# Pooled scores on quarters of the array, eight weight parts' low halves on TensorE, and a planner that counts GpSimd's hold

## The chip, the cores and the metric

The program runs on one core of one Trainium2 chip. The metric is the device time of one execution in microseconds; before the change the median of three runs is 743.98 us (743.76 to 744.39). The core has five engines with an in-order instruction queue each: TensorE (PE in the profile; its weight loads are PEld), VectorE (DVE), ScalarE (ACT), GpSimd (POOL) and SyncE (SP), which here only issues DMA transfers.

## The reference

Two stages, all in float32; some weights come as float64. Stage one is attention for 8 batches of 8 heads, 576 positions, head size 64. Each head does it twice and adds the results:

```python
q_d = q.reshape(B, H, Sd, factor, D).mean(axis=3)      # factor 4, Sd = 144; k_d, v_d alike
out_up = np.repeat(sm_attn(q_d, k_d, v_d), factor, axis=2)
mask = np.abs(pos[:, None] - pos[None, :]) < factor    # local: seven keys around each query
out_local = np.matmul(softmax(where(mask, scores, -1e9)), v)
return out_up + out_local
```

Stage two is a channel mix on x, the heads side by side (512 wide), with x_prev one position earlier:

```python
xk = mu_k * x + (1 - mu_k) * x_prev                    # xr the same with mu_r
k = np.maximum(xk @ w_k, 0); v = (k * k) @ w_v         # 512 -> 1024 -> 512
return sigmoid(xr @ w_r) * v
```

## The kernel before, in words

**Pairs.** Attention goes by 32 pairs of heads, n = 0 to 31, four to a batch; the two heads (e = 0, 1) lie in partitions 0 to 63 and 64 to 127. For a pair `turn_q` (L296) and `turn_k` (L305) transpose the raw queries and keys on VectorE. The keys go into `kz`, two planes that are zero where the other head lies, so `turn_k` is two transposes of 64 partitions, and one matmul with 128 rows gives both heads' local scores side by side. `pool_q`, `pool_k` and `pool_v` (L312 to L332) add groups of four positions on GpSimd.

**Scores.** Local scores (`ps_s`, L343) are 24 small f32 matmuls, for 24 blocks of 24 queries against 32 keys; for the first eight pairs (`PEM`) the mask is first written by a matmul with the identity (L340), later VectorE adds it. Pooled scores (`ps_d`, L400) are 144 x 144 a head, in three tiles of 64 queries a head starting at 0, 64 and 80 (`T0`); the third overlaps. Each is a matmul of 64 rows and 64 columns, head 0 on the upper left quarter of the array and head 1 on the lower right. Maxima and sums are VectorE's, exponentials ScalarE's, normalising is GpSimd's. `down_turn` (L435, L436) transposes the pooled weights on TensorE through `att` banks, `down_copy` (L444, L446) copies them out, and `av_pe` (L457, L463) multiplies by the values. `spread` (L393) fills the local weights into `bd`. From pair 5 on `run_pe` issues the values of pair n-1 and the scores of pair n as one block. The `att` ring has two banks, used by `ps_s`, `ps_d` and `ps_t`.

**Chunks.** Stage two goes by 18 chunks of 256 positions. Every product is split: an operand is a high part, rounded to fp32r, and a low part, the rest, and three products (high x high, low x high, high x low) are added. For a chunk c the mixing (`diff` L515, `mix_part`, `mix_add` L540) makes xk, `mix_high` (L544) and `mix_low` (L549) split it into `xkh` and `xkl`, `k_pe` (L557) makes eight slices `ps_g` of k, ScalarE squares them and takes the high part `kh` (L569), `k_low` (L576) makes `kl` on VectorE or GpSimd (GpSimd for chunk 0 and for slices 1, 3 and 5, `KLF`), `r_pe` (L588) makes the gate and `v_pe` (L606) the second product.

**Weights.** Twenty parts of 128 x 512 arrive as float64, 512 KB each, into staging tiles borrowed from later buffers. ScalarE scales the upper word (L224), VectorE makes a float32 of both words in three integer operations (L229, L233, L238), ScalarE rounds the high part (L242), and `weight_low` (L247) subtracts it: ten parts on VectorE (`LOWDVE`), ten on GpSimd.

**Order.** Nothing is left to a scheduler. Each step is given to `Plan.add` with its engine, a duration in us, a rank (roughly a due time, from `PER`, `STEP0`, `STEP1`, `W0`, `WSTEP`, `XLEAD`, `MIXED`), what it reads and writes, and the ring it takes a buffer from. `Plan.order` plays the steps on that model: of the steps that could start first on an engine it takes the lowest rank. The order that results is fixed on every engine. The durations in it only choose an order; they are no measurement.

Of the kernel before, what the change touches and what calls it, by code (L numbers as in the profile page):

```python
# [154 lines left out]
def attention_moe(ctx: ExitStack, tc, q, k, v, mu_k, mu_r, w_k, w_v, w_r, band, ident, out):  # L155
# [85 lines left out]
    def weight_high(i):  # L241
        nc.scalar.activation(weight_part(WORDER[i])[1], part32[i], AF.Copy)  # L242

# [54 lines left out]
    def turn_k(n):  # L298

        d = st[n]  # L300
        d["kz"] = kz = kzs[n % 2]
        raw = d["kraw"].rearrange("p c d -> p (c d)")
        for e in range(2):
            h = slice(64 * e, 64 * e + 64)
            nc.vector.transpose(kz[h, e, 3:579], raw[h])  # L305
# [21 lines left out]
    def pool_v(n):  # L327
# [4 lines left out]
        nc.gpsimd.tensor_tensor(out=vd, in0=v4[:, :, 0:64], in1=v4[:, :, 64:128], op=ALU.add)  # L332
        d["vd"] = vd

    def score_pe(n):
        d = st[n]
        qT, kz = d["qT"], d["kz"]
        ps = pp.tile([P, NG, 2, 32], F32, tag="att", name="ps_s", bufs=AB)
        if n < PEM:
            nc.tensor.matmul(ps, idn, mask[:, :, None, :].broadcast_to([P, NG, 2, 32]), start=True, stop=False)  # L340
        for j in range(4 * NG):
            g, i = divmod(j, 4)
            nc.tensor.matmul(ps[32 * i:32 * i + 32, g, :, :], qT[:, QT * j:QT * j + 32],  # L343
                             kz[:, :, QT * j:QT * j + 32], start=(n >= PEM), stop=(n >= PEM or g == NG - 1))
        d["ps_s"] = ps

    def score_top(n):
        d = st[n]
# [4 lines left out]
        if n < PEM:
            p3 = ps.rearrange("p g e c -> p (g e) c")
            nc.vector.tensor_reduce(out=mx, in_=p3, axis=AX.X, op=ALU.max)
            nc.vector.tensor_tensor(out=s3, in0=p3, in1=mx[:, :, None].broadcast_to([P, 12, 32]),
                                    op=ALU.subtract)
        else:
            nc.vector.tensor_tensor(out=sm, in0=ps, in1=mask[:, :, None, :].broadcast_to([P, NG, 2, 32]),
                                    op=ALU.add)  # L360
            nc.vector.tensor_reduce(out=mx, in_=s3, axis=AX.X, op=ALU.max)
        d.update(s3=s3, mx=mx)
# [31 lines left out]

    def down_pe(n):
        d = st[n]
        ps = pp.tile([P, 3, 144], F32, tag="g" if n < NP else "att", name="ps_d", bufs=2)
        for t in range(3):
            for e in range(2):
                nc.tensor.matmul(ps[64 * e:64 * e + 64, t, :], d["qd"][64 * e:64 * e + 64, T0[t]:T0[t] + 64],  # L400
                                 d["kd"][64 * e:64 * e + 64, :], start=True, stop=True)
        d["ps_d"] = ps

    def down_top(n):
        d = st[n]
# [1 line left out]
        nc.vector.tensor_reduce(out=mx, in_=d["ps_d"], axis=AX.X, op=ALU.max)
# [458 lines left out]
```

## Time and profile before

| | |
|---|---|
| median of three runs | 743.98 us |
| the profiled execution | 744.03 us |
| its span, first to last instruction | 742.2 us |
| mean granted TensorE clock | 0.958 |
| PE, DVE, ACT, POOL busy | 664.1, 479.7, 454.5, 332.9 us |
| DMA | 62.14 MB, mean 84 GB/s |

A row of a group reads: line, engine, operation, output and inputs by the program's names, shapes, count, then busy time and mean duration in ns of one, then the idle time of the engine ahead of it and what ended that. In the chain a row is a start, a length and a line; "x12" counts records, and an f32 matmul leaves two.

### The profile page before, as it was taken

The page shows a single profiled execution, that of the slowest core. Times are in us where ns is not written, and L with a number is a line of the kernel's source. Part 1 is how long each engine was busy: PE and PEld are TensorE (multiplying, and loading weights), DVE is VectorE, ACT ScalarE, POOL GpSimd, SP SyncE. Part 2 cuts the span into 40 slices and gives each one's busy share as a digit, 9 for nine tenths or more (in the row PEclk, how much of TensorE's full clock was granted, in tenths as well). Part 3 has the DMA queues.
Part 4 walks back from the last instruction along what each step waited for, and adds up shares of the span by engine and source line. Part 5 has one row for each costly group of instructions (what it writes and reads, how often), then busy time and mean ns, then how long its engine had stood idle before and what let it go on. Part 6 is the DMA issues. An engine that isn't in the chain of part 4 may idle for free.

```text
span 742.2 us, 17757 instructions
## 1 busy us (share of the span) xinstructions
PE 664.1 (89%) x7008; PEld 569.1 (77%) x7008; DVE 479.7 (65%) x839; ACT 454.5 (61%) x1150; POOL 332.9 (45%) x400
## 2 busy tenths in 40 slices
PE   2651777789999999999999999999999999999997
PEld 2441655668788878887888888887888788888886
DVE  3679879856885596559845387829782975175111
ACT  1365656557775767576765567657765776564432
POOL 6634547546565464543434255636563653010100
PEclk9975878799999999999999999999999999999999
DMA  9999765354336243623234143544353100000000
GB/s 136 177 236 162 174 145 138 51 130 85 87 73 127 50 99 67 123 57 79 46 86 99 39 91 59 119 54 103 66 119 59 58 2 30 1 30 29 1 28 29
DMA packets 221845, 62.14 MB, mean 84 GB/s; under 512 B 205122, under 2 KB 214594, under 8 KB 221762
## 3 DMA queue, kind: packets, MB, share of 16 engines
q1 hardware_dynamic: 221762, 61.01, 39.1%
q8 instruction: 55, 0.90, 0.5%
q14 instruction: 28, 0.23, 0.1%
HBM read 51.55 MB, written 9.44 MB: 82 GB/s over the span
## 4 chain that ended last, share of the span: by engine, by line
PE 79%; DVE 8%; DMA 3%; issue 3%; SPq 3%; ACT 2%; POOL 1%; DVEq 0%; POOLq 0%; ACTq 0%
PE ps_g L557 27%; PE acc L606 23%; PE ps_r L588 14%; PE ps_v L463 3%; PE ps_s L343 3%; PE ps_d L400 3%; PE ps_v L457 2%; SPq L259 2%; DMA qraw<-in_q_dram 2%; PE ps_t L435 1%; DVE xkl L549 1%; DVE w L238 1%; DMA stg<-in_moe_w_k_dram 1%; DVE w L233 1%; DVE xk L540 1%
## 5 line engine op out<-in xcount | busy, mean ns | idle before, releaser
L557 PE MATMUL ps_g<-xkh,wkh 128*128 128x256 f32 x576 | 167.0, 290 | 13.3 <-ACT xkh L544 11.1
L557 PE MATMUL ps_g<-xkl,wkh 128*128 128x256 f32 x576 | 164.8, 286 | 15.7 <-DVE xkl L549 15.7
L557 PE MATMUL ps_g<-xkh,wkl 128*128 128x256 f32 x576 | 163.7, 284 | 0.0
L576 POOL TENSOR_TENSOR kl<-kk,kh 128x256 fp32r<-128x256 f32 x59 | 46.9, 796 | 224.2 <-ACT kh L569 174.4
L576 DVE TENSOR_TENSOR kl<-kk,kh 128x256 fp32r<-128x256 f32 x85 | 46.9, 552 | 149.6 <-ACT kh L569 143.9
L557 PEld LDWEIGHTS ps_g<-xkl,wkh 128*128 128x128 f32 x576 | 111.0, 193 | 21.3 <-DVE xkl L549 17.8
L562 ACT ACTIVATE kk<-ps_g 128x256 f32<-128x256 f32 x144 | 55.1, 382 | 116.9 <-PE ps_g L557 110.4
L557 PEld LDWEIGHTS ps_g<-xkh,wkh 128*128 128x128 f32 x576 | 111.1, 193 | 18.8 <-ACT xkh L544 11.3
L606 PE MATMUL acc<-wvh,kh 128*128 128x512 f32 x288 | 116.3, 404 | 0.0
L606 PE MATMUL acc<-wvh,kl 128*128 128x512 f32 x288 | 114.0, 396 | 1.5 <-DVE kl L576 1.5
L606 PE MATMUL acc<-wvl,kh 128*128 128x512 f32 x288 | 113.8, 395 | 1.6 <-POOL wvl L247 1.0
L557 PEld LDWEIGHTS ps_g<-xkh,wkl 128*128 128x128 f32 x576 | 111.2, 193 | 0.0
L606 PEld LDWEIGHTS acc<-wvh,kl 128*128 128x128 f32 x288 | 54.2, 188 | 15.5 <-DVE kl L576 2.3
L393 ACT ACTIVATE bd<-at 32x288 f32<-32x288 f32 x128 | 56.2, 439 | 14.8 <-DVE at L386 13.2
L569 ACT ACTIVATE kh<-kk 128x256 fp32r<-128x256 f32 x144 | 60.2, 418 | 4.7 <-PE acc L606 0.2
L568 ACT ACTIVATE kk<-kk 128x256 f32<-128x256 f32 x144 | 60.1, 418 | 4.4
L606 PEld LDWEIGHTS acc<-wvl,kh 128*128 128x128 f32 x288 | 54.3, 189 | 10.8 <-POOL wvl L247 1.3
L606 PEld LDWEIGHTS acc<-wvh,kh 128*128 128x128 f32 x288 | 54.2, 188 | 9.7 <-issue 0.2
L588 PE MATMUL ps_r<-wrh,xrh 128*128 128x512 f32 x144 | 57.2, 397 | 0.0
L588 PE MATMUL ps_r<-wrh,xrl 128*128 128x512 f32 x144 | 56.9, 395 | 0.0
L588 PE MATMUL ps_r<-wrl,xrh 128*128 128x512 f32 x144 | 56.8, 395 | 0.0
L323 POOL TENSOR_TENSOR tk<-kz 64x288 f32<-64x288 f32 x64 | 50.1, 783 | 13.4 <-DVE kz L305 10.2
(89 smaller groups left out, 1344.0 us busy)
## 6 DMA issues: line engine op xcount, KB each, us to landing
vw<-in_v_dram SPq DMA_DIRECT2D x126, 96.0 KB
qraw<-in_q_dram SPq DMA_DIRECT2D x128, 72.0 KB
kraw<-in_k_dram SPq DMA_DIRECT2D x128, 72.0 KB
v<-in_v_dram SPq DMA_DIRECT2D x32, 288.0 KB
out_dram<-sig SPq DMA_DIRECT2D x36, 256.0 KB
stg<-in_moe_w_k_dram SPq DMA_DIRECT2D x6, 512.0 KB
stgx<-in_moe_w_v_dram SPq DMA_DIRECT2D x4, 512.0 KB
stg<-in_moe_w_v_dram SPq DMA_DIRECT2D x4, 512.0 KB
```

What stands on the lines that cost most here:

```text
L323: nc.gpsimd.tensor_tensor(out=tk[h], in0=k4[:, :, 0:2], in1=k4[:, :, 2:4], op=ALU.add)
L343: nc.tensor.matmul(ps[32 * i:32 * i + 32, g, :, :], qT[:, QT * j:QT * j + 32], kz[:, :, QT * j:QT * j + 32], start=(n >= PEM), stop=(n >= ...
L393: nc.scalar.activation(dst, src, AF.Copy)
L400: nc.tensor.matmul(ps[64 * e:64 * e + 64, t, :], d["qd"][64 * e:64 * e + 64, T0[t]:T0[t] + 64], d["kd"][64 * e:64 * e + 64, :], start=True ...
L463: nc.tensor.matmul(pv[r][64 * e:64 * e + 64, 48 * g:48 * g + 48], d["vw"][h, 6 * e + g, :], bd[h, 2 * g + e, :], start=True, stop=True)
L557: nc.tensor.matmul(ps, w[:, p, P * f:P * f + P], y[:, p, :], start=(m == 0), stop=(m == len(mm) - 1))
L562: nc.scalar.activation(kk, kq[c, f], AF.Relu)
L568: nc.scalar.activation(kk, kk, AF.Square)
L569: nc.scalar.activation(kh, kk, AF.Copy)
L576: eng.tensor_tensor(out=kl, in0=kk, in1=kh.bitcast(F32), op=ALU.subtract)
L588: nc.tensor.matmul(ps, y[:, p, P * t:P * t + P], w[:, p, :], start=(m == 0), stop=(m == len(mm) - 1))
L606: nc.tensor.matmul(accs[c][t], x[:, P * t:P * t + P], w[:, f, :], start=(f == 0 and m == 0), stop=(f == NF - 1 and m == 2))
```

## The change

- **Pooled scores.** `T0` goes. `ps_a` is one tile of two banks that holds the pooled scores of both heads and the local scores, head 0 in the first bank and head 1 in the second (`S1`, `D0`, `DP`). Queries 0 to 127 of each head are four matmuls of 64 rows and 64 columns, one on each quarter of the array by head and query half (`down_pe`); the last 16 queries of both heads are one matmul over the whole array (`down_last`), for which ScalarE copies them into a zeroed strip of `qd` (`last_q`). `down_turn` has two banks of `ps_a` (ring `att`, now one tile), before pair 4 two `g` banks, and `down_copy` is two copies instead of four.
- **Local scores of pairs 0 to 7** (`SPLIT`): 48 matmuls, one a block and head, with 64 rows. `turn_k` is then one transpose of 128 partitions and `pool_k` two additions instead of three. The mask comes by matmul for four pairs (`PEM`) instead of eight.
- **Weights.** The low parts of parts 0 to 7 (`LOWPE`: k0 to k3, v0 to v3) are made by TensorE, identity x part minus identity x high part, in banks `c0` and `c1`, and copied out by ScalarE; all other low parts are GpSimd's (`LOWDVE` is empty).
- **Other moves.** `pool_v` of pairs 0 to 3 is VectorE's. `kl` is GpSimd's only for chunk 0 and slice 3.
- **The plan.** A step of VectorE named in `SHARED` is lengthened by 0.6 of the time that it overlaps with GpSimd's work in the model; many durations and ranks change.

```diff
+S1, D0, DP = 656, 192, 160
+LOWPE = tuple(range(8))
+VDVE = 4
+SPLIT = 8
-PEM = 8
-LOWDVE = (1, 3, 5, 7, 9, 11, 13, 15, 17, 19)
+PEM = 4
+LOWDVE = ()
-KLPOOL, KLF = 1, (1, 3, 5)
+KLPOOL, KLF = 1, (3,)
-PER = 34.6
-STEP0, STEP1, W0, WSTEP = 8.0, 14.0, -20.0, 2.5
-XLEAD, MIXED = 18.0, 12.0
+PER = 33.5
+STEP0, STEP1, W0, WSTEP = 4.0, 4.0, -25.0, 2.0
+XLEAD, MIXED = 18.0, 6.0
...
+            if eng == "DVE" and t["name"] in self.SHARED:
+                us += self.PORT * max(0.0, min(s + us, free.get("POOL", 0.0)) - s)
...
+    def weight_diff(i):
+        hi = weight_part(WORDER[i])[1]
+        left[i] = ps = pp.tile([P, 512], F32, tag=f"c{i % 2}", name="ps_w", bufs=1)
+        nc.tensor.matmul(ps, idn, part32[i], start=True, stop=False)
+        nc.tensor.matmul(ps, nidn, hi, start=False, stop=True)
+    def weight_left(i):
+        nc.scalar.activation(weight_part(WORDER[i])[2], left[i], AF.Copy)
...
+        if n < SPLIT:
+            nc.vector.transpose(kz[:, 0, 3:579], raw)
+            d["k4"] = [(slice(0, P), kz[:, 0, 3:579])]
+            return
...
+    def last_q(n):
+        qd = qds[n % 2]
+        for e in range(2):
+            h = slice(64 * e, 64 * e + 64)
+            nc.scalar.activation(qd[h, 144 + 16 * e:160 + 16 * e], qd[h, 128:144], AF.Copy)
...
+        eng = nc.vector if n < VDVE else nc.gpsimd
...
+            for e in range(2):
+                h = slice(64 * e, 64 * e + 64)
+                nc.tensor.matmul(ps[32 * i:32 * i + 32, S1 * e + 32 * g:S1 * e + 32 * g + 32],
+                                 qT[h, QT * j:QT * j + 32], kz[h, 0, QT * j:QT * j + 32],
+                                 start=(n >= PEM), stop=(n >= PEM or g == NG - 1))
...
+    def down_last(n):
+        d = st[n]
+        d["ps"] = ps = pp.tile([P, 1024], F32, tag="att", name="ps_a", bufs=1)
+        nc.tensor.matmul(ps[:, D0 + DP:D0 + DP + 144], d["qd"][:, 144:272], d["kd"], start=True, stop=True)
     def down_pe(n):
         d = st[n]
-        for t in range(3):
-            for e in range(2):
-                nc.tensor.matmul(ps[64 * e:64 * e + 64, t, :], d["qd"][64 * e:64 * e + 64, T0[t]:T0[t] + 64],
-                                 d["kd"][64 * e:64 * e + 64, :], start=True, stop=True)
+        for e in range(2):
+            for h in range(2):
+                o = D0 + 2 * DP * e
+                nc.tensor.matmul(d["ps"][64 * h:64 * h + 64, o:o + 144],
+                                 d["qd"][64 * e:64 * e + 64, 64 * h:64 * h + 64], d["kd"][64 * e:64 * e + 64, :],
+                                 start=True, stop=True)
...
     def run_pe(n):
+        down_last(n)
         av_pe(n - 1)
         down_pe(n)
         score_pe(n)
...
+        if i in LOWPE:
+            add("PE", 1.5, R + 3, weight_diff, i, r=[f"w{i}", "h" + key, "nidn"], new=[(f"wd{i}", f"c{i % 2}")])
+            add("ACT", 0.64, R + 4, weight_left, i, r=[f"wd{i}"], w=["l" + key])
+            return
```

Three places show how the order moves. First TensorE, one block of a later pair (values of the pair before, scores of this pair), before and with the change:

```order
L557 MATMUL ps_g<-xkh,wkl 128x256
L457 MATMUL ps_v<-adT,vd 64x144 x4
L463 MATMUL ps_v<-bd,vw 64x48 x24
L400 MATMUL ps_d<-kd,qd 64x144 x6
L343 MATMUL ps_s<-kz_75,qT_77 32x64 x24
L606 MATMUL acc_2886<-wvh,kh 128x512
```

```order
L629 MATMUL ps_g<-xkh,wkl 128x256
L461 MATMUL ps_a<-kd,qd_75 128x144
L527 MATMUL ps_v<-adT,vd 64x144 x4
L533 MATMUL ps_v<-bd,vw 64x48 x24
L468 MATMUL ps_a<-kd,qd_75 64x144 x4
L400 MATMUL ps_a<-kz_78,qT_81 32x64 x24
```

Six pooled-score matmuls (L400 before) become one over the whole array ahead of the values (L461) and four on quarters behind them (L468); L400 with the change is the local scores.

Second VectorE, between the first and the second chunk's `xkl`; `w_...` is a weight part in the making, `wkl` a low part, before and with the change:

```order
L238 SCALAR_TENSOR_TENSOR w_898<-stg,w_898 128x512
L229 TENSOR_SCALAR w_900<-w_900 128x512
L233 SCALAR_TENSOR_TENSOR w_900<-stgx,w_900 128x512
L247 TENSOR_TENSOR wkl<-w_898,wkh 128x512
L238 SCALAR_TENSOR_TENSOR w_900<-stgx,w_900 128x512
L305 STREAM_TRANSPOSE kz_75<-kraw 64x576 x2
L229 TENSOR_SCALAR w_935<-w_935 128x512
L233 SCALAR_TENSOR_TENSOR w_935<-stgx,w_935 128x512
```

```order
L250 SCALAR_TENSOR_TENSOR w_960<-stg,w_960 128x512
L255 SCALAR_TENSOR_TENSOR w_960<-stg,w_960 128x512
L621 TENSOR_TENSOR xrl<-dx,xrh 128x1024
L246 TENSOR_SCALAR w_989<-w_989 128x512
L250 SCALAR_TENSOR_TENSOR w_989<-stg,w_989 128x512
L255 SCALAR_TENSOR_TENSOR w_989<-stg,w_989 128x512
L246 TENSOR_SCALAR w_1047<-w_1047 128x512
L250 SCALAR_TENSOR_TENSOR w_1047<-stgx,w_1047 128x512
```

No low part stands between the weight operations any more, and the transposes of the pair stand ahead of the first `xkl`.

Third GpSimd at the same place, before and with the change:

```order
L515 TENSOR_TENSOR dx<-xt 128x1024
L576 TENSOR_TENSOR kl<-kk,kh 128x256
L247 TENSOR_TENSOR wkl<-w_781,wkh 128x512
L312 TENSOR_TENSOR tq<-qT_77 128x288
L313 TENSOR_TENSOR qd<-tq 128x144
L247 TENSOR_TENSOR wkl<-w_900,wkh 128x512
```

```order
L587 TENSOR_TENSOR dx<-xt 128x1024
L648 TENSOR_TENSOR kl<-kk,kh 128x256
L274 TENSOR_TENSOR wkl<-w_989,wkh 128x512
L648 TENSOR_TENSOR kl<-kk,kh 128x256 x2
L274 TENSOR_TENSOR wkl<-w_1047,wkh 128x512
L274 TENSOR_TENSOR wkl<-w_1071,wkh 128x512
```

All of the parts from k4 on stand here, and the pooling of the next pair comes earlier or later around them.

More of the change, by code (lines that the diff above doesn't have):

```diff
@@ L164, in attention_moe @@
     idn = cp.tile([P, P], F32, name="idn")
+    nidn = cp.tile([P, P], F32R, name="nidn")
     muk = cp.tile([P, NP], F32, name="muk")
@@ L172, in attention_moe @@
     wrl = cp.tile([P, NP, DM], F32R, name="wrl")
+    qds = [cp.tile([P, 272], F32, name=f"qd{i}") for i in range(2)]
     bd = cp.tile([P, 12, 48], F32, name="bd")
     kzs = [cp.tile([P, 2, 584], F32, name=f"kz{i}") for i in range(2)]
+    mask2 = cp.tile([P, NG, 2, 32], F32, name="mask2")
     qTs = [cp.tile([P, 592], F32, name=f"qT{i}") for i in range(2)]
@@ L345, in score_pe @@
-        d["ps_s"] = ps
+            if n >= SPLIT:
+                o = S1 * (g // 3) + 64 * (g % 3)
+                nc.tensor.matmul(ps[32 * i:32 * i + 32, o:o + 64], qT[:, QT * j:QT * j + 32],
+                                 kz[:, :, QT * j:QT * j + 32], start=True, stop=True)
+                continue
+            for e in range(2):
+                h = slice(64 * e, 64 * e + 64)
+                nc.tensor.matmul(ps[32 * i:32 * i + 32, S1 * e + 32 * g:S1 * e + 32 * g + 32],
+                                 qT[h, QT * j:QT * j + 32], kz[h, 0, QT * j:QT * j + 32],
+                                 start=(n >= PEM), stop=(n >= PEM or g == NG - 1))
@@ L357, in score_top @@
                                     op=ALU.subtract)
         else:
[L359 to L362, printed above, removed]
+            to = sm if n < SPLIT else sm.rearrange("p (a g) e c -> p a (g e c)", a=2)
+            nc.vector.tensor_tensor(out=to, in0=ps, in1=wide, op=ALU.add)
+            nc.vector.tensor_reduce(out=mx, in_=sm, axis=AX.X, op=ALU.max)
@@ L406, in down_top @@
         mx = wp.tile([P, 3], F32, tag="mxd", name="mxd")
[L407 removed]
+        nc.vector.tensor_reduce(out=mx, in_=down_part(d["ps"]), axis=AX.X, op=ALU.max)
         nc.vector.tensor_scalar(out=mx, in0=mx, scalar1=-1.0 / 128, scalar2=None, op0=ALU.mult)
@@ L467, in av_banks @@
     def av_banks(n):
-        return ("acc0", "acc1") if n < NP and n % 2 == 0 else ("c0", "c1")
+        return ("acc0", "acc1") if n < NP else ("c0", "c1")
     def score_both(n):
+        down_last(n)
+        score_pe(n)
         down_pe(n)
-        score_pe(n)
     def run_pe(n):
+        down_last(n)
         av_pe(n - 1)
@@ L663, in pair_scores @@
             add("ACT", 1.76, R1 - 4, spread, n, r=[f"at{n}"], w=["bd"])
-            for kt in range(2):
-                add("PE", 0.4, R1 - 7, down_turn, n, kt, r=[f"ad{n}"], new=[(f"pst{n}{kt}", "att")])
-                add("ACT", 0.57, R1 - 6, down_copy, n, kt, r=[f"pst{n}{kt}"],
-                    new=[(f"adT{n}", "adT")] if kt == 0 else [], w=[f"adT{n}"] if kt else [])
+            add("PE", 0.65, R1 - 7, down_turn, n, r=[f"ad{n}"],
+                new=[(f"pst{n}{kt}", "g") for kt in range(2)] if n < NP else [(f"pst{n}0", "att")])
+            add("ACT", 0.85, R1 - 6, down_copy, n, r=[f"pst{n}0"] + ([f"pst{n}1"] if n < NP else []),
+                new=[(f"adT{n}", "adT")])
         if part == 2:
@@ L711, in chunk @@
         X = T - XLEAD
-        add(on, 2.4 if on == "POOL" else 1.25, X, diff, c, r=xt, new=[(f"dx{c}", "f32tmp")])
+        add(on, 2.2 if on == "POOL" else 1.1, X, diff, c, r=xt, new=[(f"dx{c}", "f32tmp")])
         for nm, o in (("xk", 0), ("xr", 5)):
@@ L715, in chunk @@
             for p in range(NP):
-                add(*(("ACT", 0.42) if act_mix(c) else ("DVE", 0.7)), X + o + 1 + 0.5 * p, mix_part, c, nm, (p,),
+                add(*(("ACT", 0.42) if act_mix(c) else ("DVE", 0.6 * len(segs(c)))), X + o + 1 + 0.5 * p, mix_part, c, nm, (p,),
                     r=xt + [f"dx{c}", "mu"] + ([f"xkh{c}"] if nm == "xr" and c < ACTMIX else []),
@@ L736, in chunk @@
                     held.pop(0)()
-            add("PE", 1.44, W, k_pe, c, f, r=[f"xkh{c}", f"xkl{c}"] + both(f"k{4 * (f // 4) + p}" for p in range(NP)),
+            add("PE", 1.43, W, k_pe, c, f, r=[f"xkh{c}", f"xkl{c}"] + both(f"k{4 * (f // 4) + p}" for p in range(NP)),
                 new=[(f"g{c}.{f}", "g")])
@@ L773, in begin_all @@
         add("SP", 1.0, -110, load_consts, w=["mask", "idn"])
-        add("POOL", 2.2, -110, clear, w=["kz0", "kz1", "qT0", "qT1", "bd"])
+        add("POOL", 2.2, -110, clear, w=["kT0", "kT1", "qT0", "qT1", "qd.0", "qd.1", "bd"])
         add("SP", 1.0, W0, load_mus, w=["mu"])
     begin_all()
+    add("ACT", 0.3, -60, turn_sign, r=["idn"], w=["nidn"])
+    add("POOL", 1.0, -60, double_mask, r=["mask"], w=["mask2"])
     for i in range(len(WORDER)):
```

143 lines of the change are left out of this document (78 added, 65 removed).

## The prediction

> **What bounds the kernel now.** I read the page's engine shares first, then the slices of the span, then a table of stretches, and only then the waits inside each stretch, because a share is an average over stages with different limits.
>
> ```profile
> span 742.2 us, 17757 instructions
> PE 664.1 (89%) x7008; PEld 569.1 (77%) x7008; DVE 479.7 (65%) x839; ACT 454.5 (61%) x1150; POOL 332.9 (45%) x400
> ...
> PE   2651777789999999999999999999999999999997
> ...
> PEclk9975878799999999999999999999999999999999
> ```
>
> TensorE (PE) is busy 89% of the span, but the slices (18.6 us each) say that this is two kernels: about eight slices in which PE is half idle and its granted clock drops, and 32 in which it is full. The table gives the borders; its columns are the start and end, the length, each engine's busy time, then clock, DMA share and GB/s.
>
> ```profile
> core 0: us, PE busy (x) PEld busy (x) DVE busy (x) ACT busy (x) POOL busy (x), PEclk, DMA share, GB/s
> 0.00:40.00 40.00, 16.72 (x266) 11.51 (x266) 20.49 (x42) 10.64 (x37) 25.33 (x41) 0.98 0.98 160
> 40.00:60.00 20.00, 11.87 (x238) 9.32 (x238) 16.35 (x35) 13.86 (x38) 7.69 (x8) 0.67 0.96 221
> 60.00:75.00 15.00, 1.61 (x6) 1.32 (x7) 14.86 (x13) 8.07 (x15) 7.85 (x6) 0.50 0.98 167
> 75.00:135.00 60.00, 40.02 (x338) 31.91 (x338) 51.68 (x73) 34.86 (x84) 36.38 (x36) 0.78 0.60 143
> 135.00:160.00 25.00, 22.81 (x221) 19.74 (x221) 18.95 (x34) 15.38 (x39) 14.61 (x19) 0.88 0.47 97
> 160.00:742.20 582.20, 571.06 (x5943) 495.33 (x5942) 357.35 (x647) 371.71 (x938) 241.04 (x291) 1.00 0.30 65
> ```
>
> Up to 40 us the DMA engines are full (share 0.98) and nothing else is. From 40 to 135 us VectorE (DVE) is the full engine: 16.35 + 14.86 + 51.68 = 82.9 of 95 us, while PE works 53.5. From 160 us PE is the limit: 571.1 of 582.2 us, clock 1.00. So an edit is worth what it takes from VectorE's queue in the second stretch, and what it takes from PE's queue in the last; elsewhere it is worth nothing. Of the 11.1 us that PE idles in the last stretch the waits name 7.5:
>
> ```profile
> PE ps_g L557 <- DVE xkl L549: 6.0, 5, 1.4
> PE acc L606 <- DVE kl L576: 1.5, 2, 0.9
> ```
>
> The border at 135 us is the second chunk's input: the chain ends with two weight operations of VectorE, the chunk's `xkl`, and then PE without a gap.
>
> ```profile
> 130.73 1.04 DVE w L238
> ...
> 133.30 1.45 DVE xkl L549
> 134.79 8.53 PE ps_g L557 x47
> ...
> 145.56 0.84 PE ps_s L340 x2
> ```
>
> **Scores on quarters (PE, last stretch).** One pair's block on PE, in the chain of one chunk:
>
> ```profile
> 392.03 0.84 PE ps_v L463 x48
> 392.87 0.75 PE ps_d L400 x12
> 393.63 0.81 PE ps_s L343 x48
> 394.43 1.60 PE acc L606 x6
> ```
>
> Each f32 matmul leaves two records. The six pooled-score matmuls on two quarters (`ps_d`) take 0.75 us, 62.5 ns a record. They become one matmul over the whole array and four on the four quarters. The whole one has no row; the mask matmul at 145.56 is f32 over the whole array too, 0.84 us for 384 columns, so 144 columns cost 0.32 at most, and 0.25 if they stream as on two quarters (twice 0.125). The four: eight records at 62.5 ns are 0.50 us if only two quarters run at a time, 0.25 if four do. `ps_v` L463 also works on four quarters, at 0.84/48 = 17.5 ns a record of 48 columns, and `ps_s` with 64 columns needs 16.9: so this is the pace of issue, not of columns, and four quarters do overlap. I take 0.28 for the four and 0.27 for the whole: 0.55, a gain of 0.20 a pair, between a loss of 0.07 and a gain of 0.25. The block starts 25 times after 160 us (300 records of `ps_d` there, twelve each):
>
> ```profile
> L400 PE MATMUL ps_d<-kd,qd 64*64 64x144 f32 x300 | 23.3, 285 | 0.0
> ```
>
> That is **5.0 us** (bounds +1.75 and -6.25). The local scores of the first eight pairs become 48 matmuls instead of 24: at the pace of issue +0.81 a pair. Pairs 0 to 3 have it while DMA sets the time; pairs 4 to 7 lose their mask matmul (0.84) for it: zero. From pair 8 on they stay. The single two-bank `ps_a` adds a wait of `down_last` for `down_copy` of the pair before; `av_pe` right behind it waited for that copy already: zero.
>
> **Low parts on TensorE, and what else leaves VectorE.** The groups of VectorE and GpSimd from 40 to 135 us:
>
> ```profile
> L229 DVE TENSOR_SCALAR w<-w 128x512 int32<-128x512 int32 x18 | 12.5, 693 | 1.9 <-ACT w L224 1.7
> L238 DVE SCALAR_TENSOR_TENSOR w<-stg,w 128x512 int32<-128x512 int32 x12 | 10.8, 903 | 0.2
> L233 DVE SCALAR_TENSOR_TENSOR w<-stgx,w 128x512 int32<-128x512 int32 x6 | 8.9, 1482 | 0.1
> L247 DVE TENSOR_TENSOR wvl<-w,wvh 128x512 fp32r<-128x512 f32 x4 | 5.4, 1343 | 2.0 <-ACT wvh L242 2.0
> L305 DVE STREAM_TRANSPOSE kz<-kraw 64x576 f32<-64x576 f32 x6 | 4.5, 754 | 0.1
> L247 DVE TENSOR_TENSOR wkl<-w,wkh 128x512 fp32r<-128x512 f32 x4 | 3.2, 801 | 0.0
> L549 DVE TENSOR_TENSOR xkl<-xk,xkh 128x1024 fp32r<-128x1024 f32 x2 | 2.7, 1330 | 0.0
> ...
> L247 POOL TENSOR_TENSOR wvl<-w,wvh 128x512 fp32r<-128x512 f32 x4 | 5.5, 1385 | 0.0
> ```
>
> No low part is left on VectorE: -5.4 - 3.2 = -8.6 us. The key transposes of a pair become one of 128 partitions; a transpose costs the same on 64 partitions as I expect on 128 (754 ns, and the queries' own 128-partition transposes in the same stretch 753):
>
> ```profile
> L296 DVE STREAM_TRANSPOSE qT<-qraw 128x576 f32<-128x576 f32 x3 | 2.3, 753 | 0.0
> ```
>
> so three pairs save 2.2. The pooled values of pairs 0 to 3 come to VectorE: 512 + 256 elements; by `xkl` (1,330 ns for 1,024) 1.0 us a pair, bounds 0.9 and 1.2 (the last by `wkl`, 801 ns for 512). Pairs 0 and 1 fall into the first 40 us, where VectorE works 20.5: hidden. Pairs 2 and 3: +2.0. Sum: -8.8. But the new order puts more ahead of the second `xkl`: the three operations of two more weights (0.42 + 0.69 + 0.69 each at their shortest, rows below: 3.6), one pair's output (0.8, below) and its transposes (1.5). So the border moves by 8.8 - 5.9 = **3.0 us** (bounds 0 and 8.8), and the 5.9 us are missing behind it. There PE lost 2.2 us idle and 25 x 0.12 = 3.0 us by its clock of 0.88; I take two thirds of 5.2, **3.5 us** (bounds 0 and 5.2).
>
> TensorE pays two matmuls for each of eight parts: f32 of 512 columns, 0.84 x 512/384 = 1.12, and one at `acc`'s pace, 1.60/6 = 0.27 at most: 1.4 us, 11 in all, twice that at clock 0.50. From 40 to 75 us PE idles 21.5 us and that hides it; only the part v3 stands between two `k_pe`, 1.4 us if its cover is gone. ScalarE pays eight copies like this one of its own, 5.0 us, where it works 21.9 of 35: hidden.
>
> ```profile
> L242 ACT ACTIVATE wkh<-w 128x512 fp32r<-128x512 f32 x8 | 5.0, 630 | 3.5 <-DVE w L238 3.4
> ```
>
> On SP's queue the windows of pair 3 now stand behind four weight loads instead of two. They are issued early:
>
> ```profile
> 32.93 3.28 SPq L282 DMA_DIRECT2D vw<-in_v_dram  x4
> ```
>
> and the pair's output comes at 58.52 (below); two loads of 512 KB more are 4.7 us at 221 GB/s: hidden.
>
> **GpSimd's hold.** These two answers, VectorE and then GpSimd, show the same 6 us:
>
> ```profile
> 58.52 0.82 DVE L494 TENSOR_TENSOR xt<-ps_v,up 128x288 f32<-128x288 f32 x2
> ...
> 60.37 4.28 DVE L233 SCALAR_TENSOR_TENSOR w<-stgx,w 128x512 int32<-128x512 int32 x1
> ...
> 65.29 0.42 DVE L229 TENSOR_SCALAR w<-w 128x512 int32<-128x512 int32 x1
> 65.74 0.69 DVE L233 SCALAR_TENSOR_TENSOR w<-stgx,w 128x512 int32<-128x512 int32 x1
> ```
>
> ```profile
> 59.97 1.05 POOL L332 TENSOR_TENSOR vd<-v 72x256 f32<-72x256 f32 x1
> ...
> 62.21 1.89 POOL L515 TENSOR_TENSOR dx<-xt 128x1024 f32<-128x1024 f32 x1
> ```
>
> The same operation takes 0.69 us alone and 4.28 until GpSimd's run ends at 64.1. The mean of L233 on `stgx` (1,482 ns) is full of that; the transposes (754 ns throughout) are not held. Before the first chunk GpSimd loses low parts and the values of pair 3; behind it the twelve remaining low parts are all GpSimd's, where six were. Up to 75 us I take back 3.5 us of hold (the 4.28 less 0.69), behind it I add 2.0: six more parts at 1.385 are 8.3 us of GpSimd, of which a quarter meets a held operation. Net **1.5 us** gained, between 3.6 gained and 4.8 lost (all 8.3 held).
>
> **Sum.** 5.0 + 3.0 + 3.5 + 1.5 = 13.0 us off the profiled execution, 744.0 us (span 742.2 and 1.8 around it; the median of the runs shown is 743.98, the same). **Forecast: 731.0 us.** Two more `kl` a chunk move from GpSimd to VectorE, 34 in 17 chunks, and the run blocks come earlier by the plan's numbers; I cost both at nothing, since VectorE has 357 of 582 us in use there.
>
> **Rivals.**
>
> *More than forecast, 714 us.* All terms at their good end, 8.8 + 5.2 + 3.6 + 6.25 = 23.9, and the 6.0 us of `xkl` waits gone with earlier runs: 744.0 - 29.9. For it: the waits are few and short. Against: GpSimd has not less to do. Chance 0.25.
>
> *The hold eats the start, 739 us.* All six added low parts hold VectorE: -4.8 instead of +1.5, and PE is late for the `v` parts by the rest of the 8.0 us. For it: the 4.28 row. Against: the plan now counts six tenths of such an overlap and orders by it. 744.0 - 5.0. Chance 0.18. The Trainium skill, GPSIMD Engine Reference, section 4.1 Engine Selection, assigns elementwise work on a tile to VectorE and calls GpSimd about twice as slow with two inputs, and its section 1 names contention for VectorE operations with two SBUF inputs. By that rule twelve low parts on GpSimd are the wrong way and the result is this rival; the trace agrees with the slowness (1,385 ns against 801) and with the contention (4.28 against 0.69).
>
> *The quarters do not run together, 738 us*: the change does not do what it says. The pooled scores cost 0.82 instead of 0.55: 744.0 - 8.0 + 1.75 = 737.8. Against it speaks `ps_v`. Chance 0.12.
>
> *Slower, 755 us.* The 34 moved `kl` stand in VectorE's in-order queue and wait for ScalarE's `kh`:
>
> ```profile
> L576 DVE TENSOR_TENSOR kl<-kk,kh 128x256 fp32r<-128x256 f32 x85 | 46.9, 552 | 149.6 <-ACT kh L569 143.9
> ```
>
> 143.9/85 = 1.7 us of idle VectorE each. If mixing and outputs queued behind come late and PE waits 0.7 us for each, that is 34 x 0.7 = 23.8 on 731. It decides from 13.0/34 = 0.38 us on. Against it: PE's whole wait for `kl` is 1.5 us. Chance 0.08.
>
> **How the numbers follow.** The forecast has 0.37. Within 0.2% (about 1.5 us, what a measurement here can tell from no change) is only a mixture of the third and fourth case: 0.04. Faster 0.87, slower 0.09. The range from 712 to 743 takes in the first three rivals and the unknown prices; left out are the slower case and a tail below.
>
> **What would show it.** Right: a pooled-score piece of some 0.28 + 0.27 us in the pair's block; the second chunk's `xkl` ending before 132 us; from there PE above 95% at clock 1.00; the weight operations still held, but later. Wrong: `ps_a` pieces near 0.8 us a pair; PE waits for `kl` of more than 10 us; the second `xkl` at 135 or later; or a gain well over 13 us, which would mean that the stretch from 40 to 135 us hung on something else than VectorE's sum of work, for example on the order alone.

## The result, and the profile after

The changed kernel takes **722.67 us** (median of four runs, 721.27 to 725.29) where the kernel before takes 744.18 (743.76 to 745.58) beside it: a ratio of 0.971, 95% interval 0.968 to 0.974. The gain is 21.5 us where 13.0 were forecast; 722.7 lies inside the range, between the forecast (731) and the first rival (714). The profiled execution took 722.32 us.

The page of the changed kernel, its engine shares and slices (18.0 us each):

```profile
span 720.5 us, 18491 instructions
PE 660.0 (92%) x7352; PEld 564.5 (78%) x7352; DVE 482.8 (67%) x863; ACT 465.0 (65%) x1159; POOL 299.4 (42%) x362
...
PE   2676785798999999999999999999999999999997
...
PEclk9977886799999999999999999999999999999999
```

TensorE's busy time fell by only 4.1 us (664.1 before) where the span fell by 21.7, so its idle time fell by 17.6; part of that is filled by work that is new on TensorE, the low parts and the split local scores. The table of stretches for the changed kernel, with the borders and columns of the prediction's table:

```profile
0.00:40.00 40.00, 18.70 (x502) 15.11 (x506) 23.33 (x49) 14.30 (x46) 19.10 (x36) 0.91 0.98 176
40.00:60.00 20.00, 14.15 (x227) 8.12 (x219) 15.66 (x31) 12.91 (x32) 3.41 (x4) 0.76 1.04 196
60.00:75.00 15.00, 7.85 (x116) 4.04 (x116) 8.86 (x13) 8.54 (x18) 6.29 (x8) 0.73 1.06 189
75.00:135.00 60.00, 43.01 (x488) 35.03 (x488) 55.36 (x70) 40.16 (x98) 45.94 (x42) 0.73 0.61 144
135.00:160.00 25.00, 24.40 (x296) 21.28 (x297) 17.39 (x36) 17.31 (x47) 16.62 (x24) 0.99 0.61 117
160.00:720.50 560.50, 551.92 (x5747) 480.88 (x5746) 362.16 (x665) 371.79 (x920) 208.06 (x251) 1.00 0.29 66
```

VectorE is no longer full from 60 to 75 us (8.86 of 15, before 14.86), and from 135 us TensorE runs at clock 0.99 where it had 0.88. One pair's block on TensorE, in the chain of waits of the changed kernel:

```profile
302.51 0.24 PE ps_a L461 x2
302.75 0.64 PE ps_v L527 x8
303.39 0.84 PE ps_v L533 x48
304.24 0.26 PE ps_a L468 x8
304.50 0.81 PE ps_a L400 x48
```

The pooled scores take 0.24 + 0.26 = 0.50 us where they took 0.75. The waits of TensorE after 160 us in the changed kernel (what waits, for what, us in total, times, longest):

```profile
PE ps_t L508 <- POOL ad L496: 3.1, 4, 1.1
PE acc L678 <- DVE kl L648: 1.2, 1, 1.2
PE ps_r L660 <- DVE sig L682: 0.6, 1, 0.6
```

The five waits for `xkl` (6.0 us before) are gone; waits for `ad`, the normalised pooled weights, are new.

**Where the lead arises.** For every kernel I counted the records of `ps_g`, `acc`, `ps_r` and `ps_v` in windows of 5 us, weighted them by the chain's pace in the last stretch (0.118 us a record of `ps_g`, 0.233 of `acc` and `ps_r`, 3.6 us a pair), and read off when each kernel had done as much as the kernel before at 160, 200, 400 and 700 us. A negative number is a lead in us, good to about 0.4, of the profiled execution. Three of these were well below the median of their kernel (e_mixed by 2.8 us, e_klf by 2.0, b_quarters by 1.9), so their leads are larger than their medians show:

```
                                             160    200    400    700
changed kernel                              -8.4   -8.0  -11.7  -20.6
changed, all old ranks (e_ranks)           -10.4   -5.0   -0.3   +2.2
changed, old ranks of the start (e_hyb)     -3.6   -0.5   -3.6   -7.9
changed, old PER and MIXED (e_hyb2)         -4.5   -4.8   -1.4   +0.5
changed, MIXED 12 alone (e_mixed)           -5.2   -6.4   -3.0   -3.4
changed, PER 34.6 alone (e_per)             +0.1   -2.5   -4.9  -14.3
changed, PORT 0 (e_port)                    -5.3   -4.5   -7.0  -13.8
changed, low parts as before (e_lowdve)     -5.5   -6.7  -11.0  -17.3
changed, SPLIT and PEM 0 (e_split0)         -1.3   +2.0   -0.1   -7.2
changed, kl as before (e_klf)               -9.6  -10.4  -12.9  -21.3
before, new ranks alone (b_ranks)           +3.9   +1.8   -2.5   -9.7
before, new ranks and scores (b_quarters)   -6.2   -8.5   -9.9  -17.0
```

So the changed kernel wins 8.0 us by 200 us, and 12.6 more in the 500 us behind. The prediction had 8.0 (3.0 + 3.5 + 1.5) for the first part and 5.0 for the second.

### The profile page after: what moved, and what is told of

Its sections match the earlier page's. It is cut to its first block, busy times and chain, and to the rows that moved or that the text cites. A ratio compares the mean times of both kernels' runs of the same rounds, so it can differ in the third digit from the quotient of the medians.

```text
span 720.5 us, 18491 instructions
## 1 busy us (share of the span) xinstructions
PE 660.0 (92%) x7352; PEld 564.5 (78%) x7352; DVE 482.8 (67%) x863; ACT 465.0 (65%) x1159; POOL 299.4 (42%) x362
## 4 chain that ended last, share of the span: by engine, by line
PE 76%; DVE 7%; ACT 4%; POOL 4%; DMA 3%; SPq 3%; issue 1%; POOLq 0%; ACTq 0%; DVEq 0%
PE ps_g L629 25%; PE acc L678 23%; PE ps_r L660 14%; PE ps_v L533 3%; PE ps_a L400 3%; PE ps_v L527 3%; SPq L286 2%; PE ps_a L461 1%; DMA v<-in_v_dram 1%; DMA stgx<-in_moe_w_k_dram 1%; ACT ad L485 1%; PE ps_a L468 1%; ACT L485 1%; PE ps_t L508 1%; DVE mxd L475 1%
## 5 line engine op out<-in xcount | busy, mean ns | idle before, releaser
L629 PE MATMUL ps_g<-xkl,wkh 128*128 128x256 f32 x576 | 162.5, 282 | 0.7 <-DVE xkl L621 0.7
L629 PE MATMUL ps_g<-xkh,wkl 128*128 128x256 f32 x576 | 162.0, 281 | 0.0
L648 DVE TENSOR_TENSOR kl<-kk,kh 128x256 fp32r<-128x256 f32 x119 | 65.9, 554 | 95.8 <-ACT kh L641 90.0
L428 POOL TENSOR_TENSOR sm<-sm,mx 128x384 f32<-128x384 f32 x28 | 28.2, 1007 | 98.5 <-DVE mx L423 81.6
L648 POOL TENSOR_TENSOR kl<-kk,kh 128x256 fp32r<-128x256 f32 x25 | 21.2, 850 | 110.8 <-PE acc L678 81.3
L678 PEld LDWEIGHTS acc<-wvl,kh 128*128 128x128 f32 x288 | 54.9, 190 | 11.7 <-POOL wvl L274 3.1
L475 DVE TENSOR_REDUCE mxd<-ps_a 128x3 f32<-128x432 f32 x32 | 19.4, 606 | 61.9 <-PE ps_a L400 56.9
```

The lines of the kernel that those rows point to most:

```text
L428: nc.gpsimd.tensor_tensor(out=s3, in0=s3, in1=mx[:, :, None].broadcast_to([P, 12, 32]), op=ALU.subtract)
L475: nc.vector.tensor_reduce(out=mx, in_=down_part(d["ps"]), axis=AX.X, op=ALU.max)
L629: nc.tensor.matmul(ps, w[:, p, P * f:P * f + P], y[:, p, :], start=(m == 0), stop=(m == len(mm) - 1))
L648: eng.tensor_tensor(out=kl, in0=kk, in1=kh.bitcast(F32), op=ALU.subtract)
L678: nc.tensor.matmul(accs[c][t], x[:, P * t:P * t + P], w[:, f, :], start=(f == 0 and m == 0), stop=(f == NF - 1 and m == 2))
```

## The experiments

The kernels were run in three groups; the kernel before ran beside each and took 743.07, 742.52 and 742.41 us. Ratios are against it, with 95% intervals. Each diff is against the changed kernel, except in the second.

**1. All old ranks in the changed kernel.**

```diff
-PER = 33.5
-STEP0, STEP1, W0, WSTEP = 4.0, 4.0, -25.0, 2.0
-XLEAD, MIXED = 18.0, 6.0
+PER = 34.6
+STEP0, STEP1, W0, WSTEP = 8.0, 14.0, -20.0, 2.5
+XLEAD, MIXED = 18.0, 12.0
```

> The changed kernel with the old ranks (PER 34.6, STEP0 8, STEP1 14, W0 -20, WSTEP 2.5, MIXED 12), all else as changed. Theory A: the gain has three parts, about 8 us up to 200 us because VectorE's queue is shorter, 25 blocks x 0.25 = 6.2 us by the quarters, and some 6 to 7 us after 200 us because the new ranks bring each chunk's xkl earlier, so that TensorE's 6.0 us of waits for it vanish. Then the old ranks bring these waits back: 728 to 730 us, with more than 4 us of PE waits for xkl after 160 us. Theory B: the waits vanish because the plan counts GpSimd's hold. Theory C: they vanish because GpSimd has less to do (kl of two slices moved). Under B and C: 722 to 724 us and no waits for xkl.

Measured: 746.88 us, ratio 1.0064 (1.0041 to 1.0087). Without its ranks, the change as a whole makes the kernel slower. The 10.4 us of lead that it has at 160 us are lost by 400. TensorE's waits after 160 us:

```profile
PE ps_g L629 <- DVE xkl L621: 5.5, 5, 1.9
PE acc L678 <- DVE kl L648: 5.1, 5, 1.2
PE ps_t L508 <- POOL ad L496: 4.4, 7, 0.7
PE ps_g L629 <- ACT xkh L616: 3.6, 1, 3.6
```

The five `xkl` waits are back. The direction was that of the theory of the ranks; the loss against the changed kernel, 0.0352 of 743 or 26 us, was far more than that theory had put down.

**2. The new ranks alone in the kernel before.**

```diff
-PER = 34.6
-STEP0, STEP1, W0, WSTEP = 8.0, 14.0, -20.0, 2.5
-XLEAD, MIXED = 18.0, 12.0
+PER = 33.5
+STEP0, STEP1, W0, WSTEP = 4.0, 4.0, -25.0, 2.0
+XLEAD, MIXED = 18.0, 6.0
```

> The kernel before with the new ranks alone. Theory A (the ranks take away the waits for xkl after 160 us): 737 to 739 us. Theories B and C (they do not): 743 to 746 us, the waits for xkl still 5 to 7 us.

Measured: 732.57 us, 0.9860 (0.9845 to 0.9876). Six numbers, and no other edit, win 10.5 us. All of it comes after 200 us, where this kernel is 1.8 us behind. The direction is that of Theory A, the size is more than it said, and B and C, which expected no gain here, are out. TensorE's only named wait after 160 us is one of 2.2 us:

```profile
PE ps_g L557 <- ACT sig L597: 2.2, 1, 2.2
```

**3. The plan does not count GpSimd's hold.**

```diff
-    PORT = 0.6
+    PORT = 0.0
```

> The changed kernel with PORT = 0, so that the plan counts no hold of GpSimd on VectorE. Theory A: the count only reorders the start, 722 to 725 us. Theory B (the count takes the waits away): 728 to 731 us, with waits of PE for xkl or for weights.

Measured: 729.69 us, 0.9817 (0.9802 to 0.9831). The counting is worth 0.0105 of 743, 8 us, about half of it by 200 us. The weight operations of VectorE from 40 to 135 us in this kernel (L246, L250, L255; 13.5 + 11.7 + 10.9 + 9.9 + 9.0 = 55.0 us) are 4.0 us longer than in the changed kernel (51.0, rows below); 0.7 of that is one operation more.

**4. Low parts as before:** ten on VectorE, ten on GpSimd, none on TensorE.

```diff
-LOWPE = tuple(range(8))
-LOWDVE = ()
+LOWPE = ()
+LOWDVE = (1, 3, 5, 7, 9, 11, 13, 15, 17, 19)
```

> The changed kernel with the low parts as before: ten on VectorE, ten on GpSimd, none on TensorE. Theory A: VectorE gets 8.6 us of work back between 40 and 135 us and GpSimd's first parts hold it again; TensorE loses 11 us of matmuls that were hidden. 727 to 731 us, all of it lost before 200 us. Theory D: the low parts are free wherever they stand and the start is set by order and transfers: 722 to 724 us.

Measured: 725.74 us, 0.9766 (0.9751 to 0.9780). This edit, which by the prediction took 8.6 of the 8.8 us off VectorE's queue, is worth 4 us (0.0054 of 743), between what the two theories said. It takes only two parts off GpSimd (ten for twelve); twelve low parts on VectorE were not tried.

**5. Old ranks of the start alone** (the weights, the first four pairs, the end of the first batch).

```diff
-STEP0, STEP1, W0, WSTEP = 4.0, 4.0, -25.0, 2.0
+STEP0, STEP1, W0, WSTEP = 8.0, 14.0, -20.0, 2.5
```

> The changed kernel with the old ranks of the start (STEP0 8, STEP1 14, W0 -20, WSTEP 2.5) and the new PER and MIXED. Known so far, against 743 us of the kernel before on one chip: all old ranks 746.9, the new ranks alone in the kernel before 732.6. Theory A: PER and MIXED place the runs and with them xkl earlier and take away TensorE's stalls after 200 us; the ranks of the start are worth little, and the old ones even had the kernel 4 us further at 180 us. Then 717 to 721 us. Theory E: the ranks of the start set the phase of everything behind, and the old ones bring the stalls back: above 738 us.

Measured: 735.82 us, 0.9905 (0.9883 to 0.9927). Nearly the whole lead at 200 us goes (0.5 left of 8.0), with not one operation more on any engine, and 5.2 us more are missing at 700 us. Theory A, by which these four numbers are worth little, is out; E's 738 is not reached.

**6. Old PER and MIXED, new start.**

```diff
-PER = 33.5
-XLEAD, MIXED = 18.0, 6.0
+PER = 34.6
+XLEAD, MIXED = 18.0, 12.0
```

> The complement: new ranks of the start, old PER 34.6 and MIXED 12. Theory A: the stalls after 200 us come back, 742 to 750 us. Theory E: 721 to 725 us.

Measured: 742.97 us, 0.9999 (0.9984 to 1.0013). With these two numbers old, nothing of the gain is left. The next two runs take them apart.

**7. MIXED alone.** In the plan a batch is due `MIXED` after the time of the chunk that precedes the first one to need it, and that first one begins its mixing `XLEAD` = 18 ahead of its own time; chunks are `PER` apart. With 6 a batch is due 9.5 us of the plan's time ahead of that mixing (33.5 - 6 - 18), with 12 only 3.5.

```diff
-XLEAD, MIXED = 18.0, 6.0
+XLEAD, MIXED = 18.0, 12.0
```

> The changed kernel with MIXED at 12.0 again (each batch's pairs may end 6 us later against the chunk that needs them), PER left at 33.5. What is still open: PER and MIXED back together cost 20 to 21 us over the change's 722; which of the two? Theory A (the late end of a batch alone makes xkl late): MIXED alone brings back most of it, 738 us, with PE waits for xkl of 4 us and more after 160 us. Theory B (the spacing PER decides): MIXED alone costs little, 725 us. Theory C (any other phase of pairs against chunks is worse, no single number carries it): each alone costs 5 to 15 us and the two don't add up to 21, about 731 us.

Measured: 743.10 us, 1.0000 (0.9984 to 1.0017). Theory A holds: this one number costs 0.0288 of 743, 21 us, more than A had said. At 200 us the profiled execution is still 6.4 us ahead; at 400 it has 3.0 left. Its waits of TensorE after 160 us:

```profile
PE ps_t L508 <- POOL ad L496: 6.7, 9, 1.1
PE ps_g L629 <- DVE xkl L621: 4.7, 5, 1.9
PE acc L678 <- DVE kl L648: 4.4, 5, 1.3
```

Named waits explain 15.8 us against 4.9 in the changed kernel. The chain of this kernel through the longest of the five `xkl` waits shows what stands behind them:

```profile
317.61 0.85 PE ps_a L400 x48
...
318.48 0.62 DVE mxd L475
...
319.40 1.28 ACT L485
...
324.54 1.29 ACT xk L598 x3
...
327.65 1.91 DVE xk L612 x2
...
329.90 1.20 DVE dx L612 x2
...
331.95 1.17 DVE xkl L621
...
333.17 0.85 PE ps_g L629 x5
```

From 318.5 to 333.2 us the time is set by ScalarE and VectorE: the pair's exponentials, and then the mixing of the next chunk, in one in-order row behind a pair that came too late for it. In the changed kernel the chain at this place (300 to 330 us) holds nothing but TensorE. TensorE's own timeline shows what that costs it. Up to 329.1 us its matmuls follow each other at the full pace (`ps_g` every 0.12 us, `acc` every 0.23), and then come two gaps:

```profile
329.95 0.50 PE L678 MATMUL acc<-wvh,kl 128*128 128x512 f32 x1 [0.43 <-DVE kl L648]
...
333.17 0.39 PE L629 MATMUL ps_g<-xkl,wkh 128*128 128x256 f32 x1 [1.90 <-DVE xkl L621]
```

A named wait is a little too short: a record of a matmul of `ps_g` lasts some 280 ns where its pace in the chain is 1.41 us for 12, 118 ns, so of each gap some 0.16 us counts as busy. That gives an estimate of the whole loss. Behind 160 us the profiled execution falls 14.8 us behind the changed kernel's (18.0 in the span, 3.2 of it by 160 us). Named waits are 15.8 us here and 4.9 there, 10.9 more; 13 waits more (19 against 6) hide some 2.1; 1.8 us are left without a row.

**8. PER alone.**

```diff
-PER = 33.5
+PER = 34.6
```

> The changed kernel with PER at 34.6 again (pairs and chunks both spaced wider by 3 percent against the fixed steps of the start and the fixed leads), MIXED left at 6.0. Theory A (MIXED decides): little cost, 725 us. Theory B (PER decides): 738 us, with PE waits for xkl of 4 us after 160 us. Theory C (phase, no single number): 731 us.

Measured: 729.57 us, 0.9825 (0.9809 to 0.9842). It costs 8 us, at the other end: 5.5 of the lead at 200 us, and little of the gain behind. No `xkl` wait comes back after 160 us. With MIXED at 12 the same edit costs nothing more (runs 6 and 7), so the numbers do not add, as Theory C had it.

**9. The kernel before with the new ranks and the new scores:** `ps_a`, quarters, one matmul for the last queries, but no unloading of VectorE. The mask of all pairs is added by VectorE.

```diff
-LOWPE = tuple(range(8))
-VDVE = 4
-SPLIT = 8
-PEM = 4
-LOWDVE = ()
-KLPOOL, KLF = 1, (3,)
+LOWPE = ()
+VDVE = 0
+SPLIT = 0
+PEM = 0
+LOWDVE = (1, 3, 5, 7, 9, 11, 13, 15, 17, 19)
+KLPOOL, KLF = 1, (1, 3, 5)
-    PORT = 0.6
+    PORT = 0.0
```

> The pooled scores on quarters with the one ps_a buffer and the new ranks, everything else as before (low parts ten on VectorE and ten on GpSimd, pooled values on GpSimd, kl of slices 1, 3, 5 on GpSimd, no hold counted, local scores of all pairs by 24 matmuls); only the mask is added by VectorE for all pairs. To compare with the new ranks alone, 732.6 against 743. Theory A: 25 blocks x 0.25 us = 6.2 us less, 725 to 728 us, all of it after 160 us. Theory F: the single buffer puts each pair's chain of exponentials ahead of TensorE's transposes and takes the gain back: 730 to 735 us, with more than 4 us of PE waits for the normalised weights.

Measured: 728.41 us, 0.9806 (0.9776 to 0.9835), between the two theories. Against run 2 the new scores win 0.0054, 4.0 us, with an uncertainty of some 2.5, so the 6.2 of Theory A are not excluded. What they may give back shows in the waits of TensorE after 160 us; run 2 has no wait for `ad`:

```profile
PE ps_t L508 <- POOL ad L496: 4.0, 3, 2.2
```

And this kernel, with ten low parts and all key transposes of 64 partitions still on VectorE, is 8.5 us ahead at 200 us (6.6 if its execution's 1.9 us below the median all lie there), about as much as the changed one.

**10. Local scores of all pairs in 24 matmuls, mask by VectorE.**

```diff
-SPLIT = 8
-PEM = 4
+SPLIT = 0
+PEM = 0
```

> The changed kernel with the first eight pairs' local scores done as the later ones' (two key transposes of 64 partitions, 24 matmuls, mask added by VectorE). Theory A: VectorE gets 0.75 us a pair back, 3 us in its full stretch, and GpSimd three additions instead of two a pair: 724 to 727 us, lost before 200 us. Theory D: VectorE's sum of work between 40 and 135 us does not set the start, since with the old ranks the second xkl came 9 us earlier and the kernel was not faster: 721 to 723 us.

Measured: 734.52 us, 0.9879 (0.9851 to 0.9907). Both theories had expected far less: the whole lead of the start goes, and 2.0 us more. One wait of TensorE between 40 and 160 us, in this kernel, is as long as that:

```profile
PE ps_w L266 <- ACT wvh L259: 10.3, 1, 10.3
```

TensorE's queue is in order: a low part that stands in it waits for its weight, and everything behind waits with it. In the changed kernel the same wait is 2.9 us (two times). But this wait is not shown to be the loss. It ends at 76.6 us, and the first chunk's products begin behind it at 78.15 where the changed kernel begins them at 74.79, so it can explain 3.4 of the 10 us; and run 9 has a wait of 11.7 us before its first chunk, for `xkh`, and keeps its lead. Where the rest goes was not taken apart.

**11. kl as before,** slices 1, 3 and 5 on GpSimd.

```diff
-KLPOOL, KLF = 1, (3,)
+KLPOOL, KLF = 1, (1, 3, 5)
```

> The changed kernel with slices 1, 3 and 5 of kl on GpSimd in chunks 1 to 17 (KLF as before), so the 34 kl that moved to VectorE go back. The prediction costed that move at nothing: then 722 us, within 1.5 us. Rival 'slower by the moved kl': undoing it gains, 715 us or less. A third way: GpSimd, whose normalising now follows closer on the pair's block, is late with ad, and PE waits for ad 5 us and more after 160 us: 727 us.

Measured: 723.68 us, 0.9739 (0.9720 to 0.9757), which overlaps the changed kernel's interval. The moved `kl` cost nothing, as forecast; a gain of 1 us is within the noise.

**12. PER a little lower,** a try at a better version.

```diff
-PER = 33.5
+PER = 33.0
```

> The changed kernel with PER at 33.0 instead of 33.5, a try at a better version. If the gain after 200 us comes from runs that end earlier against the chunk that needs them (theory A or B above), a little more of it gives little more, since no wait for xkl is left: 721 us, between 719 and 723. If the result is a matter of phase (theory C), it may go either way by 5 us and more, to 727 or more at the worse end.

Measured: 723.59 us, 0.9742 (0.9727 to 0.9757). No better, and just outside the 719 to 723 that were expected; its waits after 160 us are those of the changed kernel (`ad` 3.1, `kl` 1.2, `sig` 0.6). None of the runs beats the changed kernel.

## Why the prediction was right, and where it was wrong

**Quarters: right.** The step took 0.28 + 0.27 us; measured are 0.26 + 0.24, so the gain is 0.25 a pair, the good bound: 6.2 us by the pieces for 25 pairs. The rival in which the quarters do not run together (0.82 a pair) is out. In the whole time 4.0 us of it arrive, give or take 2.5 (run 9).

**The single `ps_a` tile at zero: wrong, by up to 4 us.** The step said that `av_pe` waited for the same copy anyway. The copy indeed adds no named wait, but `down_turn` now waits for `ad`: 4.0 us in run 9, none in run 2, 3.1 in the changed kernel. All twelve kernels with the one tile have this wait behind 160 us (1.5 us in run 3, 6.7 in run 7), and the two without it have none. Whether the one tile makes it or the new place of the steps was not taken apart; a layout with the scores of both heads in one bank, which would leave room for two tiles, was not tried.

**The second chunk's `xkl` 3.0 us earlier: wrong in its mechanism.** The rows of the changed kernel (the timeline of VectorE, then the chain):

```profile
131.52 1.30 DVE L621 TENSOR_TENSOR xkl<-xk,xkh 128x1024 fp32r<-128x1024 f32 x1
```

```profile
129.85 0.85 PE ps_a L461 x2
...
133.82 1.15 PE ps_a L405 x74
134.97 1.92 PE ps_g L629 x12
```

`xkl` ends at 132.8, 1.9 us earlier than before (134.75), and not before 132. But TensorE begins the chunk at 134.97, where before it was 134.79: the border has not moved at all, because TensorE is at the block of a pair until then and no longer waits for `xkl`. What has changed is what lies ahead of it. Up to 135 us both kernels had done as many products (97 and 98 records of `ps_g`, 48 of `acc`). But the stretch tables of one line alone, the local values (48 records a pair; L463 before, then L533 in the changed kernel), differ:

```profile
0.00:135.00 135.00, 7.61 (x240) 6.43 (x240) 0.79 0.81 162
```

```profile
0.00:135.00 135.00, 6.72 (x288) 5.91 (x288) 0.79 0.83 166
```

Six pairs instead of five are done, and a pair is worth 3.6 us.

**TensorE's loss from 135 to 160 us: right.** 3.5 of 5.2 us were to come back; idle time and clock now lose 0.6 + 25 x 0.01 = 0.85, so 4.35 came. One pair more and 4.35 us give the lead of about 8. Behind 160 us TensorE is at 551.9 of 560.5 us and clock 1.00, as foretold.

**GpSimd's hold, a gain of 1.5: about nothing came, and one half was mis-sized.** VectorE's weight operations from 40 to 135 us in the changed kernel:

```profile
L246 DVE TENSOR_SCALAR w<-w 128x512 int32<-128x512 int32 x19 | 13.9, 730 | 4.3 <-ACT w L241 4.3
L255 DVE SCALAR_TENSOR_TENSOR w<-stg,w 128x512 int32<-128x512 int32 x12 | 10.6, 883 | 0.3
L250 DVE SCALAR_TENSOR_TENSOR w<-stgx,w 128x512 int32<-128x512 int32 x8 | 9.4, 1175 | 0.3
L250 DVE SCALAR_TENSOR_TENSOR w<-stg,w 128x512 int32<-128x512 int32 x11 | 8.6, 784 | 0.3
L255 DVE SCALAR_TENSOR_TENSOR w<-stgx,w 128x512 int32<-128x512 int32 x8 | 8.5, 1064 | 0.3
```

They are 51.0 us for 58 operations, 16.1 over the shortest (0.42, 0.69 and 0.69 for the three of a part); before it was 47.0 for 54, 14.6 over. So on them the hold grew by 1.5 us; the two `xk`, `dx` and `xkl` in the same stretch became 1.7 us shorter (9.1 to 7.4). Taken apart at 75 us, the weight operations were 6.1 over the shortest ahead of it and are 1.9 now: the 3.5 us that the prediction took back came. Behind it 8.5 became 14.3: 5.8 more, where the prediction added 2.0 because it let only a quarter of GpSimd's longer work meet a held operation. Still the plan that counts the hold gains 8 us (run 3): against the same work ordered without it, the weight operations are 3.3 us shorter beyond the one operation more.

**VectorE's sum of work as the bound of the start: wrong.** Its work there fell from 82.9 to 79.9 us of 95 only. Runs 5, 9 and 10 refute the reason itself: the old start ranks lose the lead with the same work; the kernel with ten low parts and the old transposes, whose VectorE works 90.4 us there, has it; and run 10, whose VectorE works only 74.0, does not. What these runs leave is the order in which the in-order queues meet, but which meeting costs what is not shown. That 8.0 us were forecast and 8.0 came is luck and no merit of the step. The prediction had named this way to be wrong ("the order alone").

The Trainium skill, GPSIMD Engine Reference, section 4.1 Engine selection, would keep the low parts off GpSimd. The groups of GpSimd from 40 to 135 us in the changed kernel agree that they are dear there:

```profile
L274 POOL TENSOR_TENSOR wvl<-w,wvh 128x512 fp32r<-128x512 f32 x4 | 6.9, 1722 | 1.2 <-PE ps_g L629 1.2
L274 POOL TENSOR_TENSOR wkl<-w,wkh 128x512 fp32r<-128x512 f32 x4 | 6.6, 1642 | 4.0 <-ACT wkh L259 4.0
L274 POOL TENSOR_TENSOR wrl<-w,wrh 128x512 fp32r<-128x512 f32 x4 | 5.4, 1340 | 1.3 <-ACT wrh L259 1.3
```

That is 18.9 us, 1,575 ns each, and half of the chain from 89 to 130 us lies on GpSimd. But run 4 (ten on VectorE, ten on GpSimd, none on TensorE) is 4 us slower, which says little of GpSimd, since it keeps ten of the twelve there. With 8.0 us won by 200 us, the rival "the hold eats the start" is out.

**Run blocks earlier, costed at nothing: the step that failed.** The prediction set the earlier blocks aside in half a sentence beside the `kl` move, and left the 6.0 us of `xkl` waits to a rival with 0.25. Run 2 shows 10.5 us for the new ranks alone, run 7 shows 21 us for one of the six in the changed kernel. Of the 12.6 us after 200 us, 5.5 are the quarters (22 pairs at 0.25). TensorE's idle time there falls by 3.2 us (9.6 to 6.4): the `xkl` waits are gone, the `ad` waits are new. About 4 us, by estimate, are something that no wait shows: the matmuls follow each other faster. From 200 us on, uninterrupted records of `ps_g` start 117.9 ns apart on average in the kernel before and 116.5 in the changed one, `acc` 232.8 and 231.0, `ps_r` 233.3 and 231.7; with 1,480, 760 and 360 records that is 4.0 us, and the three parts make 12.7. The granted clock is 1.00 in both. This pace goes with the four start numbers: the three kernels with the old ones (before, e_ranks, e_hyb) have 117.8 to 117.9 for `ps_g`, the eleven with the new ones 116.2 to 116.5. Run 5, with the old start numbers and the new PER and MIXED, lacks 5.2 us of the gain behind 200 us, and this pace is some 4 of them. Why the pace differs is not shown.

Less idle time and the faster pace also make up run 2: TensorE idles 5.8 us less after 200 us (9.6 to 3.8), and the pace gives some 6 (its `ps_r` is at 227.7), together the 11.5 us that it wins there. So the earlier blocks remove the waits, as run 7 shows, but that is only about half of what the new ranks gained in run 2. Why run 7 costs twice what run 2 gains is not settled: in the changed kernel the late batches also meet more waits for `ad` and `kl` (11.1 us against 4.3), which the kernel before, with the same late batches, has not (1.5).

**The moved kl at nothing: right** (run 11), and the slower rival, which hung on it, is out.

## What to carry to other kernels

Where queues are in order, a change of the numbers that set the order is a change of its own: price it first, by the waits at the seams where one stage hands to the next (here `xkl`, five times), and try the numbers alone on the kernel before, and the edits alone with the old numbers. A sum of busy time names the full engine but not what it is worth to unload it; ask instead which work is late at the border. A long wait that ends a stretch is a suspect and not yet the loss: compare it with a kernel that has such a wait and is not slower. And named idle time is not the whole difference of a matmul engine: compare how many matmuls it gets done, kind by kind, and the distance from one start to the next.
